# Strassen's algorithm for blocks 1 and 2 in the first layer's a and b products, with a ring of seven weight tiles

## The chip, the cores and the metric

The kernel runs on one core of a Trainium2 chip. The metric is the device time of one execution in microseconds (us); lower is better. Engines: PE (TensorE) multiplies, DVE (VectorE), ACT (ScalarE) and POOL (GpSimd) work on elements, SP (SyncE) issues DMAs. PSUM holds the results of matmuls, SBUF all other tiles.

## The reference

An attention within chunks of 64 tokens, then two layers over 2304 tokens of width 512. Weights of the first layer arrive in 64-bit floats.

```python
x = attention(q, k, v)                        # softmax in chunks of 64, (2304, 512)
x = (x @ w_a) * (x @ w_b) @ w_out             # first layer, d_ff = 1536
p = domain_probs / (domain_probs.sum(-1, keepdims=True) + 1e-09)
for e in range(4):                            # second layer, 4 experts, d_ff = 1024
    out += p[:, e:e+1] * (np.maximum(x @ w1[e], 0) @ w2[e])
```

## The kernel before

Tokens stand in 18 tiles of 128, in five blocks: block 0 has two tiles (256 columns), blocks 1 to 4 have four (512 columns). Each factor of a product is kept as a high and a low float32r part; ACT makes the high part by a cast (`split_hi`), POOL or DVE the low part by a subtraction (`sub_hi`), and one product is three matmuls.

**First layer.** d_ff is cut into 12 chunks f of 128, taken in pairs F = 0 to 5. For a block and a chunk, `ab_steps` makes a (12 matmuls of up to 512 columns), copies it to SBUF (`end_a`, ACT), makes b (12 matmuls), and `end_b` multiplies b out of PSUM by a (DVE) and splits the product g into gh (ACT) and gl (POOL). `x2_steps` then multiplies gh and gl of both chunks by w_out, in four steps (one for each 128 columns of the width) of 6 matmuls, and adds each out of PSUM to the block's sum xacc (DVE). The x2 of a block is put between the steps of the block behind it. F=0 runs in `spans` between the last steps of the attention, F=1 to 5 loop over the blocks in the order 1, 2, 3, 4, 0.

**Weights.** A piece is a 128x512 tile of w_a (0), w_b (1) or w_out (2) of a chunk; it is loaded into one of two raw buffers. `prep_begin` turns the 64-bit words into float32 (`from_f64`): two ACT passes, three DVE passes (L143, L144, L147), a POOL addition (L155), and the next load. `prep_end` splits the result into a tile of the ring `w_p` of eight: ACT cast, POOL subtraction. The places of these steps are written out by hand in `put(u, s, ...)`: behind step s of the u-th block.

**Second layer.** For 16 groups (four experts, four of each), `seq` makes the first product of two blocks by Strassen's algorithm (Winograd's form): 7 half products (`half_mm`, 6 matmuls) in place of 8, from combinations T1 to T4 of the blocks' tiles (B11, B21, B12, B22; `combos`) and sums S1 to S4 of the weights' quarters (`w_sums`), with five additions on DVE that combine the results. The combinations of blocks 1 and 2 are made from xacc in F=5 (`in_turn(in_place(...))`).

Each engine takes its instructions in program order. PSUM has two rings of four buffers: pm for a, b and the Strassen products, ps for x2 and others.

```python
def add_sb(out, in0, in1, op=ALU.add):        # DVE, both inputs in SBUF
    nc.vector.scalar_tensor_tensor(
        out=out, in0=in0, scalar=1.0, in1=in1, op0=ALU.mult, op1=op
    )
```

Of the kernel before, what the change touches and what calls it, by code (L numbers as in the profile page):

```python
# [28 lines left out]
def fused_kernel(  # L29
# [22 lines left out]

    nc = tc.nc
# [17 lines left out]
    w_p = ctx.enter_context(tc.tile_pool(name="w", bufs=8))  # L71
# [6 lines left out]
    st_p = early.enter_context(tc.tile_pool(name="st", bufs=3))  # L78
    late = {}
# [39 lines left out]
    pieces = [(0, f, i) for f in range(2 * NP1) for i in range(3)]  # L119
# [44 lines left out]
    def split_w(src):  # L164
        t = w_tile()
# [91 lines left out]


# [212 lines left out]
    def x2_steps(fs, j, i0, nt):  # L471
# [4 lines left out]
        def step(dd):  # L476
# [98 lines left out]
    def seq(w, t, on):  # L575
# [142 lines left out]
    with tc.manual_schedule():  # L718
# [52 lines left out]
        slots_by = [7, 9, 11, 13, 14, 15, 17, 19, 21, 21, 21]  # L771
        x2 = []
        for r, (f, j, i0, nt) in enumerate(spans):
# [7 lines left out]
            for i, step in enumerate(steps):  # L781
# [6 lines left out]
                if r > 5 and i in (3, 6):  # L788
                    if r in (6, 7):
                        (prep_begin if i == 3 else prep_end)()  # L790
                    elif r == 9 or i == (6 if r == 8 else 3):
                        prep_begin()
                if r == 10 and i in (5, 7):
                    prep_end()
            if r == 3:
                domain_probs()
        early.close()
        late["p"] = ctx.enter_context(tc.tile_pool(name="late", bufs=1))


        for F in range(1, NP1):
            T = {}
# [4 lines left out]
            put(0, 9, prep_end)
            put(0, 10, prep_end)
            if F < NP1 - 1:
                for u, s in ((0, 14), (1, 4), (2, 4), (2, 14), (3, 4), (3, 14)):  # L810
                    put(u, s, prep_begin)
                for u, s in ((1, 10), (1, 14), (4, 6), (4, 12)):
                    put(u, s, prep_end)
            else:
                w_next = w2_steps(0, True)
                for u, s in ((1, 8), (1, 14), (4, 6), (4, 12)):
                    put(u, s, lambda: w_next.pop(0)())
                at = [(1, 10 + 2 * i) for i in range(4)] + [(2, 10 + 2 * i) for i in range(5)]
                at += [(3, 2 * i) for i in range(7)] + [(4, 2), (4, 4)]
                for (u, s), go in zip(at, in_turn(in_place(acc[1], acc[2])), strict=True):  # L820
                    put(u, s, go)
            for u, j in enumerate((1, 2, 3, 4, 0)):
                nt = blocks[j][1]
                steps = [x for f in (2 * F, 2 * F + 1) for x in ab_steps(f, j, 0, nt)]
                for i, go in enumerate(x2):
                    steps.insert((2 if u else 1) * i + (8 if u == 4 else 5), go)
                x2 = x2_steps((2 * F, 2 * F + 1), j, 0, nt)
                for s, step in enumerate(steps):
                    step()
                    for go in T.get((u, s), ()):  # L830
                        go()
# [102 lines left out]
```

## Time and profile before

| | us |
|---|---|
| median of 3 runs (lowest to highest) | 1262.83 (1262.13 to 1263.19) |
| the profiled execution | 1262.41 |
| its span, first to last instruction | 1260.6 |
| PE busy in the span | 1249.0 |
| DVE, ACT, POOL busy | 689.1, 439.1, 326.6 |
| one turn of F (F=2 to 4) | 74.04 |

The profile is one execution. Busy time of an engine doesn't count issuing, branches or semaphores. Idle time is put down to what ended it; idle time of an engine that isn't the last one due costs nothing. Matmuls overlap, so a row's mean time of a matmul is longer than what it adds to a stream of them. In the rows below a is the tile of the first product and of g, gl and gh are its parts, w the weight tiles, t and raw a weight on its way out of 64 bits, s the weight sums.

### The profile page before, as it was taken

Reading aid. Unit: us, or ns where it says so; the run is one execution under the profiler, and the core shown is the slowest. Engines: PE = TensorE matmul, PEld = TensorE weight load, DVE = VectorE, ACT = ScalarE, POOL = GpSimd, SP = SyncE. Lnnn points to the kernel's source line nnn. Section 1 sums busy time; section 2 is a strip of 40 time slices with the busy share of each in tenths; the row PEclk is TensorE's granted clock in tenths of the full one; section 3 lists DMA queues with packets and bytes.
Section 4 is the critical chain, followed back from the end, with each engine's and each line's share of the span. In section 5 each row is a group of like instructions: output and inputs, shape, how many; then the busy total and the mean of one; then the engine's idle time right before and its main releaser. Section 6 shows DMA issues by size and latency. Waiting matters only on the chain.

```text
span 1260.6 us, 17511 instructions
## 1 busy us (share of the span) xinstructions
PE 1249.0 (99%) x6916; PEld 1042.6 (83%) x6916; DVE 689.1 (55%) x1124; ACT 439.1 (35%) x715; POOL 326.6 (26%) x264
## 2 busy tenths in 40 slices
PE   8999999999999999999999999999999999999998
PEld 5887888888888878888888888888888888888887
DVE  7855234343434335566666556665585556555565
ACT  4644422232222223222222232222264444444442
POOL 4523433333343343333333222232320000000000
PEclk9999999999999999999999999999999999999999
DMA  7731211111111100345443454435574444444543
GB/s 259 235 90 57 67 51 34 39 62 34 51 34 51 34 1 1 101 146 201 148 174 134 160 191 158 159 134 183 202 256 161 151 159 158 151 161 140 167 135 132
DMA packets 48033, 156.35 MB, mean 124 GB/s; under 512 B 5456, under 2 KB 5456, under 8 KB 47952
## 3 DMA queue, kind: packets, MB, share of 16 engines
q1 hardware_dynamic: 47952, 155.25, 36.5%
q8 instruction: 54, 0.88, 0.3%
q14 instruction: 27, 0.22, 0.1%
HBM read 100.18 MB, written 55.05 MB: 123 GB/s over the span
## 4 chain that ended last, share of the span: by engine, by line
PE 89%; DVE 0%; POOL 0%; ACT 0%; issue 0%
PE ps L700 31%; PE pm L566 24%; PE pm L452 20%; PE ps L413 5%; PE ps L414 5%; PE ps L415 5%; DVE s L99 0%; POOL cB L107 0%; DVE oacc L687 0%; POOL w L107 0%; POOL gl L107 0%; DVE xacc L95 0%; ACT w L92 0%
## 5 line engine op out<-in xcount | busy, mean ns | idle before, releaser
L700 PE MATMUL ps<-w,h 128*128 128x512 f32 x1536 | 353.4, 389 | 0.0
L700 PEld LDWEIGHTS ps<-w,h 128*128 128x128 f32 x1536 | 288.2, 188 | 59.8
L687 DVE SCALAR_TENSOR_TENSOR oacc<-ps,pr,oacc 128x512 f32<-128x512 f32 x270 | 191.7, 749 | 104.4 <-PE ps L700 104.4
L452 PE MATMUL pm<-xh,w 128*128 128x512 f32 (+1 forms) x976 | 232.6, 367 | 0.0
L452 PEld LDWEIGHTS pm<-xh,w 128*128 128x128 f32 x976 | 172.1, 189 | 30.6
L566 PE MATMUL pm<-cT,w 128*128 128x512 f32 x768 | 184.9, 389 | 0.0
L566 PEld LDWEIGHTS pm<-cT,w 128*128 128x128 f32 x768 | 144.0, 188 | 29.8
L566 PE MATMUL pm<-cB,w 128*128 128x512 f32 x576 | 146.6, 390 | 0.0
L107 POOL TENSOR_TENSOR w<-raw,w 128x512 fp32r<-128x512 f32 x64 | 82.6, 1290 | 203.4 <-ACT w L92 139.4
L452 PE MATMUL pm<-xl,w 128*128 128x512 f32 (+1 forms) x488 | 123.8, 366 | 1.4 <-DVE xl L99 1.4
L566 PEld LDWEIGHTS pm<-cB,w 128*128 128x128 f32 x576 | 107.0, 188 | 21.4
L107 POOL TENSOR_TENSOR gl<-a,gh 128x512 fp32r<-128x512 f32 (+1 forms) x61 | 71.2, 1168 | 188.8 <-ACT gh L92 188.7
L195 ACT CAST w<-kept 128x1024 fp32r<-128x1024 f32 x96 | 98.9, 1045 | 56.5 <-DMA kept<-kept 56.1
L95 DVE TENSOR_TENSOR xacc<-ps,xacc 128x512 f32<-128x512 f32 (+1 forms) x112 | 70.6, 633 | 87.8 <-PE ps L415 87.6
L92 ACT CAST gh<-a 128x512 fp32r<-128x512 f32 (+1 forms) x61 | 34.8, 571 | 198.9 <-DVE a L95 198.9
L452 PEld LDWEIGHTS pm<-xl,w 128*128 128x128 f32 x488 | 87.2, 189 | 16.9 <-DVE xl L99 1.6
L95 DVE TENSOR_TENSOR a<-pm,a 128x512 f32<-128x512 f32 (+1 forms) x61 | 38.4, 629 | 101.3 <-PE pm L452 98.9
L413 PE MATMUL ps<-gl,w 128*128 128x512 f32 (+1 forms) x244 | 90.3, 370 | 2.0 <-POOL gl L107 1.8
L414 PE MATMUL ps<-gh,w 128*128 128x512 f32 (+1 forms) x244 | 89.3, 366 | 0.0
L415 PE MATMUL ps<-gh,w 128*128 128x512 f32 (+1 forms) x244 | 89.0, 365 | 0.0
L155 POOL TENSOR_TENSOR t<-t,raw 128x512 int32<-128x512 int32 x36 | 46.8, 1301 | 86.0 <-issue 38.8
L107 POOL TENSOR_TENSOR w<-s,w 128x512 fp32r<-128x512 f32 x32 | 43.7, 1384 | 73.2 <-ACT w L92 73.2
(87 smaller groups left out, 1333.5 us busy)
## 6 DMA issues: line engine op xcount, KB each, us to landing
kept<-w SPq DMA_DIRECT2D x96, 512.0 KB, 6.2
kept<-kept SPq DMA_DIRECT2D x96, 512.0 KB, 3.2
raw<-in_w1p_dram SPq DMA_DIRECT2D x36, 512.0 KB, 3.5
raw<-in_w2p_dram SPq DMA_DIRECT2D x32, 512.0 KB, 4.6
q<-in_q_dram SPq DMA_DIRECT2D x18, 256.0 KB, 4.3
k<-in_k_dram SPq DMA_DIRECT2D x18, 256.0 KB, 4.7
v<-in_v_dram SPq DMA_DIRECT2D x18, 256.0 KB, 4.4
out_dram<-oacc SPq DMA_DIRECT2D x18, 256.0 KB, 2.0
```

The costliest lines, as they stand in the source:

```text
L92: nc.scalar.copy(out=dst, in_=src)
L95: nc.vector.tensor_tensor(out=out, in0=in0, in1=in1, op=op)
L107: eng.tensor_tensor(out=dst, in0=src, in1=hi.bitcast(F32), op=ALU.subtract)
L155: nc.gpsimd.tensor_tensor(out=t.bitcast(I32), in0=t.bitcast(I32), in1=low.bitcast(I32), op=ALU.add)
L195: nc.scalar.copy(out=t, in_=fetched.pop(key))
L413: nc.tensor.matmul(out=ps[:, :n], lhsT=wh, rhs=al, start=(m == 0), stop=False)
L414: nc.tensor.matmul(out=ps[:, :n], lhsT=wh, rhs=ah, start=False, stop=False)
L415: nc.tensor.matmul(out=ps[:, :n], lhsT=wl, rhs=ah, start=False, stop=(m == last))
L452: nc.tensor.matmul(out=st[i][:, :n], lhsT=x, rhs=y, start=m == 0, stop=m == 3 * KD - 1)
L566: nc.tensor.matmul(out=ps, lhsT=x, rhs=y, start=first and kk == 0 and m == 0, stop=kk == 1 and m == 2, skip_group_check=not first,)
L687: nc.vector.scalar_tensor_tensor(out=o, in0=ps, scalar=p1, in1=o, op0=ALU.mult, op1=ALU.add)
L700: nc.tensor.matmul(out=ps[k], lhsT=x[:, s], rhs=y, start=f == 0 and m == 0, stop=f == 1 and m == 2,)
```

## The change

Blocks 1 and 2 leave the plain loop in F=1 to 5. Their a and b products are made as one pair pass, "A" (`seq_ab`, 14 steps): `seq` runs once for a and once for b, with 7 x 6 matmuls each, its results C11, C22, C21, C12 being chunk and block (the first digit the chunk of the pair, the second the block). `on_b` multiplies; only C11 is still in PSUM then, the other three are in SBUF and take `add_sb`. The x2 of both blocks, eight steps, stand between the steps of the piece behind the pass. The order of the pieces is 3, 4, 0, A in F=1, then 3, 4, A, 0, and A, 3, 4, 0 in F=5. In a plain block the order is a of both chunks, then b of both.

The weights' sums S1 to S4 are made for each F and product (`sums`, four DVE additions of 256 columns) and split (`ent_s`: two ACT casts, two POOL subtractions of 512). The pieces are loaded by kind: a, a, b, b, w_out, w_out of the pair. The combinations T1 to T4 of blocks 1 and 2 are made once, in F=1, from the high and low parts of x (`first_combos`, 16 steps in blocks 3, 4 and 0). The x of blocks 1 and 2 is stored by halves of the width, high and low of each half, as `seq` wants it. The ring of weight tiles has seven tiles in place of eight; a, gl and the Strassen temporaries share a ring `ag` of six, gh has four named tiles, and the T tiles and S tiles lie in a pool `mid` that is opened when the attention's pools close and closed after A in F=5.

```diff
-    w_p = ctx.enter_context(tc.tile_pool(name="w", bufs=8))
+    w_p = ctx.enter_context(tc.tile_pool(name="w", bufs=7))
...
-    pieces = [(0, f, i) for f in range(2 * NP1) for i in range(3)]
+    pieces = [(0, f, i) for f in range(2) for i in range(3)]
+    pieces += [(0, 2 * F + f, i) for F in range(1, NP1) for i in range(3) for f in range(2)]
...
+    def begin_f32(F, i):
+
+        prep_begin()
+        f32s[F, i] = ready[0, 2 * F + i % 2, i // 2]
+
+    def sums(F, m):
+        a1, a2 = f32s[F, 2 * m], f32s[F, 2 * m + 1]
+        f32s[F, "s", m] = w_sums(a1[:, :256], a1[:, 256:], a2[:, :256], a2[:, 256:])
+
+    def ent_s(F, m, i):
+
+        t = late["mid"].tile([P, 2, 512], F32R, tag="S", name="S", bufs=2)
+        split_w(f32s[F, "s", m][i], t)
...
-    def a_tile(dtype=F32, shape=(P, 512)):
-        return g_p.tile(list(shape), dtype, tag="a", name="a", bufs=2)
...
+    def ag_tile(dtype=F32):
+        return g_p.tile([P, 512], dtype, tag="ag", name="ag", bufs=6)
...
+        steps = [
+            lambda: (temps("mT4", "ab"), temps("mT2", "cd"), whole("a", "B12", g)),
+            lambda: whole("b", "B22", g),
+            lambda: minus("c", "b", "a"),
+            later("T3", 0, lambda: two("c"), v),
+            later("T3", 1, lambda: two("c"), v),
+            lambda: whole("d", "B11", v),
+            lambda: minus("a", "a", "d"),
+            later("T1", 0, lambda: two("a"), g),
+            later("T1", 1, lambda: two("a"), g),
+            lambda: minus("b", "b", "a"),
+            later("T2", 0, lambda: two("b"), v),
+            later("T2", 1, lambda: two("b"), v),
+            lambda: whole("a", "B21", v),
+            t4,
+            later("T4", 0, lambda: tmp["e"], g),
+            later("T4", 1, lambda: tmp["e"], g),
+        ]
...
+        def on_b(name, ap):
+            g = ga[name]
+            (add if name == "11" else add_sb)(g, ap, g, ALU.mult)
+            f, j = 2 * F + (name[0] == "2"), int(name[1])
+            gs[f, j, 0] = (gh_tile(name), ag_tile(F32R))
+            to_parts(g, *gs[f, j, 0])
...
+                put(3, 8, prep_end)
+                put(3, 9, lambda: begin_f32(F, 4))
+                put(3, 12, lambda: begin_f32(F, 5))
+                put(3, 14, prep_end)
+                put(4, 1, prep_end)
...
+                    put(3, 11, lambda: begin_f32(F, 4))
+                    put(3, 13, lambda: begin_f32(F, 5))
+                    put(3, 15, prep_end)
+                    put(4, 2, prep_end)
...
+                put(0, 0, lambda: sums(n, 0))
+                put(0, 2, lambda: ent_s(n, 0, 0))
+                put(0, 3, lambda: begin_f32(n, 2))
+                put(0, 4, prep_end)
+                put(0, 5, lambda: ent_s(n, 0, 1))
+                put(0, 6, lambda: begin_f32(n, 3))
+                put(0, 8, prep_end)
+                put(0, 11, lambda: sums(n, 1))
+                put(0, 12, prep_end)
...
-            for u, j in enumerate((1, 2, 3, 4, 0)):
+            for j in ("A", 3, 4, 0) if end else (3, 4, 0, "A") if F == 1 else (3, 4, "A", 0):
+                if j == "A":
+                    steps = seq_ab(F)
+                    after = [2, 3, 4, 5]
```

Two places of the order. On POOL, in F=1 before the change, while blocks 1 and 2 run: gl are low parts of products, w of weight tiles, t the end of a conversion.

```order
L107 TENSOR_TENSOR gl<-a,gh 128x512
L107 TENSOR_TENSOR w<-t,w 128x512 x3
L107 TENSOR_TENSOR gl<-a,gh 128x512
L155 TENSOR_TENSOR t<-t,raw 128x512
L107 TENSOR_TENSOR gl<-a,gh 128x512
L155 TENSOR_TENSOR t<-t,raw 128x512
L107 TENSOR_TENSOR gl<-a,gh 128x512
L107 TENSOR_TENSOR w<-t,w 128x512 x2
L107 TENSOR_TENSOR gl<-a,gh 128x512
L155 TENSOR_TENSOR t<-t,raw 128x512
L107 TENSOR_TENSOR gl<-a,gh 128x512
```

The two w in a row are for the next pair of chunks. After the change, on POOL in F=1 while blocks 3 and 4 run; tmp and cT belong to the combinations, ag to the low parts of products:

```order
L677 TENSOR_TENSOR tmp<-cB_869 128x1024
L677 TENSOR_TENSOR tmp<-cB_870 128x1024
L109 TENSOR_TENSOR w<-t,w 128x512
L158 TENSOR_TENSOR t<-t,raw 128x512
L109 TENSOR_TENSOR ag<-ag,gh 128x512
L158 TENSOR_TENSOR t<-t,raw 128x512
L109 TENSOR_TENSOR w<-t,w 128x512
L109 TENSOR_TENSOR ag<-ag,gh 128x512
L109 TENSOR_TENSOR w<-t,w 128x512
L109 TENSOR_TENSOR cT_2174<-tmp,cT_2174 128x512 x2
L109 TENSOR_TENSOR ag<-ag,gh 128x512 x2
```

The last two rows of w ahead of the cT rows are the w_out tiles of this F, which the x2 of block 3 takes in block 4, with the low part of a product between them; two passes of 1024 and two rows of cT stand around them. On DVE, in F=2 before the change, at the turn from block 1 to block 2 (xacc_873 is the sum of block 1, filled by its x2):

```order
L95 TENSOR_TENSOR a<-pm,a 128x512
L143 TENSOR_SCALAR raw<-raw 128x512
L144 TENSOR_SCALAR t<-t 128x512
L147 SCALAR_TENSOR_TENSOR t<-t,raw 128x512
L95 TENSOR_TENSOR xacc_873<-ps,xacc_873 128x512 x3
L95 TENSOR_TENSOR a<-pm,a 128x512
L95 TENSOR_TENSOR xacc_873<-ps,xacc_873 128x512
L95 TENSOR_TENSOR a<-pm,a 128x512
L143 TENSOR_SCALAR raw<-raw 128x512
L144 TENSOR_SCALAR t<-t 128x512
L147 SCALAR_TENSOR_TENSOR t<-t,raw 128x512
```

One conversion (L143, L144, L147) stands ahead of the first addition to xacc. After the change, at the end of F=2's pair pass and in block 0 behind it (s are weight sums of F=3, xacc_882 is block 1's sum, L101 reads only SBUF, ag<-gh,ag is the end multiplication; L146, L147 and L150 are the L143, L144 and L147 of before):

```order
L101 SCALAR_TENSOR_TENSOR ag<-gh,ag 128x512
L97 TENSOR_TENSOR gh<-gh,ps 128x512
L101 SCALAR_TENSOR_TENSOR ag<-gh,ag 128x512
L97 TENSOR_TENSOR gh<-pm,gh 128x512
L101 SCALAR_TENSOR_TENSOR ag<-gh,ag 128x512
L101 SCALAR_TENSOR_TENSOR s_3033<-t 128x256
L101 SCALAR_TENSOR_TENSOR s_3032<-t 128x256
L101 SCALAR_TENSOR_TENSOR s_3032<-s_3033,t 128x256
L101 SCALAR_TENSOR_TENSOR s_3033<-t,s_3032 128x256
L146 TENSOR_SCALAR raw<-raw 128x512
L147 TENSOR_SCALAR t<-t 128x512
L150 SCALAR_TENSOR_TENSOR t<-t,raw 128x512
```

Three multiplications, four sums and a conversion have come ahead of the first addition to xacc of block 1; the conversion was there before.

## Rows read from the trace of the kernel before

**Rows 1.** The page of the kernel before: busy us of each engine over the span (share, instructions), and the chain that ended last by engine and by line.
```profile
PE 1249.0 (99%) x6916; PEld 1042.6 (83%) x6916; DVE 689.1 (55%) x1124; ACT 439.1 (35%) x715; POOL 326.6 (26%) x264
...
PE 89%; DVE 0%; POOL 0%; ACT 0%; issue 0%
PE ps L700 31%; PE pm L566 24%; PE pm L452 20%; PE ps L413 5%; PE ps L414 5%; PE ps L415 5%; DVE s L99 0%; POOL cB L107 0%; DVE oacc L687 0%; POOL w L107 0%; POOL gl L107 0%; DVE xacc L95 0%; ACT w L92 0%
```

**Rows 2.** The windows of the core: start and end of the stretch, its length, then busy us (and instructions) of PE, PEld, DVE, ACT and POOL, the granted clock of PE, the DMA share and GB/s. The first is in the attention, then F=2 and F=5.
```profile
20.00:40.00 20.00, 17.35 (x286) 14.92 (x290) 18.37 (x40) 9.67 (x19) 12.11 (x12) 0.83 0.72 243
...
219.42:293.46 74.04, 74.04 (x362) 62.68 (x361) 29.41 (x48) 21.16 (x38) 27.15 (x23) 1.00 0.14 43
...
441.54:515.20 73.66, 72.88 (x347) 61.01 (x346) 32.91 (x40) 20.86 (x33) 26.47 (x19) 1.00 0.07 22
```

**Rows 3.** The chain that ended last, in order of time: start, us, engine and line, number of instructions. The first row is a and b products of the first pair of chunks, late in the attention, the second the Strassen pass of one group of the second layer.
```profile
128.78 10.88 PE pm L452 x48
...
542.32 9.55 PE pm L566 x42
```

**Rows 4.** The waits of PE over the whole span: what it waited for, us in total, times, the longest.
```profile
PE ps L413 <- POOL gl L107: 1.8, 3, 0.8
```

**Rows 5.** The groups by form from 121 to 515 us (F=1 to 5 and the end of F=0): busy us, mean ns of one, then the idle time before them and what ended it.
```profile
L107 POOL TENSOR_TENSOR gl<-a,gh 128x512 fp32r<-128x512 f32 x43 | 55.8, 1298 | 135.6 <-ACT gh L92 135.6
L95 DVE TENSOR_TENSOR xacc<-ps,xacc 128x512 f32<-128x512 f32 x80 | 55.2, 690 | 66.0 <-PE ps L415 65.9
...
L107 POOL TENSOR_TENSOR w<-t,w 128x512 fp32r<-128x512 f32 x28 | 35.8, 1293 | 14.3 <-ACT w L92 9.1 <-issue 5.1
...
L95 DVE TENSOR_TENSOR a<-pm,a 128x512 f32<-128x512 f32 x42 | 29.1, 692 | 78.1 <-PE pm L452 75.7 <-ACT a L458 1.7
L92 ACT CAST gh<-a 128x512 fp32r<-128x512 f32 x42 | 26.1, 620 | 169.5 <-DVE a L95 169.5
...
L143 DVE TENSOR_SCALAR raw<-raw 128x512 uint32<-128x512 uint32 x27 | 19.1, 707 | 53.8 <-ACT t L141 53.7
L147 DVE SCALAR_TENSOR_TENSOR t<-t,raw 128x512 uint32<-128x512 uint32 x27 | 18.7, 692 | 0.9
...
L144 DVE TENSOR_SCALAR t<-t 128x512 f32<-128x512 f32 x27 | 11.3, 417 | 0.0
...
L107 POOL TENSOR_TENSOR gl<-a,gh 128x256 fp32r<-128x256 f32 x10 | 7.4, 737 | 30.6 <-ACT gh L92 30.6
...
L107 POOL TENSOR_TENSOR cB<-xacc,cB 128x1024 fp32r<-128x1024 f32 x2 | 5.0, 2494 | 0.0
...
L99 DVE SCALAR_TENSOR_TENSOR xacc<-xacc,xacc 128x1024 f32<-128x1024 f32 x3 | 3.7, 1217 | 0.0
...
L99 DVE SCALAR_TENSOR_TENSOR s<-s,raw 128x256 f32<-128x256 f32 x1 | 0.4, 411 | 0.0
```

**Rows 6.** The page's costliest groups: low parts of weight sums in the second layer and in F=5.
```profile
L107 POOL TENSOR_TENSOR w<-s,w 128x512 fp32r<-128x512 f32 x32 | 43.7, 1384 | 73.2 <-ACT w L92 73.2
```

**Rows 7.** The timeline in F=2: start, us, engine, line, instruction, and the idle time before it with its releaser. Words of a weight (raw, t) on DVE beside the low part of a product on POOL.
```profile
223.02 1.29 POOL L107 TENSOR_TENSOR gl<-a,gh 128x512 fp32r<-128x512 f32 x1 [3.26 <-ACT gh L92]
...
223.54 1.06 DVE L143 TENSOR_SCALAR raw<-raw 128x512 uint32<-128x512 uint32 x1 [1.25 <-ACT t L141]
...
224.52 0.41 DVE L144 TENSOR_SCALAR t<-t 128x512 f32<-128x512 f32 x1
```

**Rows 8.** The timeline in the second layer, same columns.
```profile
559.48 2.39 DVE L99 SCALAR_TENSOR_TENSOR gl<-xacc,xacc 128x512 f32<-128x512 f32 x2
559.88 3.14 POOL L107 TENSOR_TENSOR w<-s,w 128x512 fp32r<-128x512 f32 x2 [4.73 <-ACT w L92]
```

**Rows 9.** The timeline of F=5 at the wait of 0.78 us, same columns.
```profile
460.10 1.29 POOL L107 TENSOR_TENSOR gl<-a,gh 128x512 fp32r<-128x512 f32 x1 [5.77 <-ACT gh L92]
...
460.57 3.64 DVE L99 SCALAR_TENSOR_TENSOR s<-raw 128x256 f32<-128x256 f32 x2
...
461.35 2.59 POOL L107 TENSOR_TENSOR cB<-xacc,cB 128x1024 fp32r<-128x1024 f32 x1
...
464.14 0.41 DVE L99 SCALAR_TENSOR_TENSOR s<-s,raw 128x256 f32<-128x256 f32 x1
...
464.58 0.62 ACT L92 CAST w<-s 128x512 fp32r<-128x512 f32 x1 [3.61 <-DVE s L99]
...
465.28 1.30 POOL L107 TENSOR_TENSOR w<-s,w 128x512 fp32r<-128x512 f32 x1 [1.35 <-ACT w L92]
...
466.54 2.40 POOL L107 TENSOR_TENSOR cB<-xacc,cB 128x1024 fp32r<-128x1024 f32 x1
...
468.89 1.28 POOL L107 TENSOR_TENSOR gl<-a,gh 128x512 fp32r<-128x512 f32 x1
...
470.23 0.50 PE L413 MATMUL ps<-gl,w 128*128 128x512 f32 x1 [0.78 <-POOL gl L107]
```

**Rows 10.** The timeline of PE from 20 to 26.5 us, the rows with idle time before them, same columns.
```profile
20.27 0.69 PE L287 MATMUL pm<-k,q 64*64 64x64 f32 x32 [0.79 <-DMA k<-in_k_dram]
...
23.87 0.39 PE L452 MATMUL pm<-xl,w 128*128 128x256 f32 x1 [1.37 <-DVE xl L99]
...
24.82 0.74 PE L287 MATMUL pm<-k,q 64*64 64x64 f32 x30 [0.31 <-DVE d L299]
26.05 0.69 PE L322 MATMUL ps<-ident,d 128*128 128x128 f32 x2 [0.49 <-POOL d L316]
```

More of the change, by code (lines that the diff above doesn't have):

```diff
@@ L162, in w_tile, with split_w @@
         return w_p.tile([P, 2, 512], F32R, tag="w", name="w")
[L164 to L165 removed]
+    def split_w(src, t=None):
+        t = w_tile() if t is None else t
         split_hi(t[:, 0, :], src)
@@ L651, in emit_h0 @@
         w = wts[1, g]
-        hh, hl = (a_tile(F32R, (P, 2, B0)) for _ in range(2))
-        h, l = xp[0]
+        hh, hl = (late["p"].tile([P, 2, B0], F32R, tag=n, name=n) for n in ("hh0", "hl0"))
+        h, l = xp[0][0]
         for f, names in enumerate((("A11", "A12"), ("A21", "A22"))):
@@ L787, in fused_kernel @@
                     x_lo_rest()
[L788 to L794, printed above, removed]
+                for go in T.get((r, i), ()):
+                    go()
             if r == 3:
                 domain_probs()
-        early.close()
@@ L822, in fused_kernel @@
-            for u, j in enumerate((1, 2, 3, 4, 0)):
[L823 to L827, printed above, removed]
+                at = [(3, 11 + i) for i in range(4)] + [(3, 15), (4, 0), (4, 2), (4, 4), (4, 6)]
+                at += [(4, 8), (4, 10), (4, 12), (4, 14), (4, 15)] + [(0, 2 * i + 1) for i in range(4)]
@@ new lines, in fused_kernel @@
+            for j in ("A", 3, 4, 0) if end else (3, 4, 0, "A") if F == 1 else (3, 4, "A", 0):
+                if j == "A":
+                    steps = seq_ab(F)
+                    after = [2, 3, 4, 5]
+                else:
+                    nt = blocks[j][1]
+                    s0, s1 = (list(ab_steps(f, j, 0, nt)) for f in (2 * F, 2 * F + 1))
+                    steps = s0[:4] + s1[:4] + s0[4:] + s1[4:]
+                    first = 4 if j == 3 else 5
+                    after = [min(first + i * (1 if j == 3 else 2), 14) for i in range(len(x2))]
+                    if j == 0:
+                        after = [5 + i * (1 if len(x2) > 4 else 2) for i in range(len(x2))]
+                if end and j == 3:
+                    place = dict(B11="s1", B21="s2", T3="s3", T2="s4", T1="s5", T4="s6", B22="s7")
+                    for (u, s), go in zip(at, in_turn(in_place(acc[1], acc[2])), strict=True):
+                        put(u, s, go)
@@ L833, in fused_kernel @@
+                if end and j == "A":
+                    mid.close()
+                    late["p"] = ctx.enter_context(tc.tile_pool(name="late", bufs=1))
         side = []
```

189 lines of the change are left out of this document (148 added, 41 removed).

## The prediction

> **What bounds the kernel now.** I read the page's busy shares and its chain by engine first [rows 1]: TensorE (PE) is busy 99% of the span and holds 89% of the chain, so in every stage matmuls set the end, and a change pays by taking matmuls away or costs by making PE wait. The windows of one turn of the loop F come next [rows 2]: F=2 takes 74.04 us with PE busy all of it, GpSimd (POOL) 27.15 and VectorE (DVE) 29.41; only F=5 has a hole, 73.66 us with 72.88 busy. A 512-column matmul costs its stream time: 48 in a row take 10.88 us, which is 226.7 ns each, and the Strassen pass of the second layer, which is what the change brings in here, runs at the same price, 9.55 for 42 [rows 3]. The waits say how thin the cover is: PE waits for low parts out of POOL three times, 1.8 us in all, 0.8 at most [rows 4]. So POOL's queue is the second in line, although it is busy only 37% of a turn.
>
> **The saving.** For each F from 1 to 5 and for each of a and b, blocks 1 and 2 take 7 half products of 6 matmuls, 42, where 2 chunks x 2 blocks x 12 = 48 stood. That is 12 fewer in an F and 60 in all, at 226.7 ns: **-13.6 us**. A turn becomes 74.04 - 2.72 = 71.3 us. The price is sure, since both forms of the matmul run at it [rows 3]; nothing else is removed from PE. All other edits (three stores of x by halves, renamed tiles, the order of loads) change no count on PE, and with 1.00 granted clock and DMA shares of 0.07 to 0.14 in these windows [rows 2] I cost the loads at nothing: the two raw buffers are reloaded as before, some 6 per F.
>
> **What is added beside PE.** Durations are from the groups by form [rows 5]. In an F: eight weight sums of 256 columns on DVE (0.41 each, 3.3), three end multiplications that now read only SBUF instead of PSUM (0.69 each), ten more additions out of PSUM (0.69), four casts on ACT (0.62) and four low parts of sums on POOL. For those the nearest row is w<-s, 1.38 on the page's mean [rows 6]; 5.5 us. Once, in F=1 and its way in, the combinations T1 to T4 are made: on POOL two whole additions of 1024 columns (2.5 each, as cB) and four lows of 512 (1.29), on DVE five passes of 1024 (1.22) and six of 512. POOL's sum for a turn is then 27.15 + 5.5 = 32.7 of 71.3 us; DVE's grows from 29.4 to about 40 (ten additions 6.9, the sums 3.3). By busy time alone all of this hides, and the saving would stand nearly whole. The question is whether it comes in time.
>
> **DVE and POOL take turns.** A DVE instruction that reads only SBUF does not run beside one of POOL. Where POOL starts the low part gl at 223.02 for 1.29 us, DVE's mask (L143), due at 223.54, takes 1.06 in place of the 0.4 that its twin L144 takes next, and ends 0.29 after POOL's end [rows 7]. Two subtractions of 512 columns take 2.39 while POOL makes two w, and these take 3.14 in place of 2.58 [rows 8]; two sums of 256 take 3.64, not 0.83, while POOL makes gl and then cB [rows 9]. The additions out of PSUM stay at 0.69 in every group [rows 5]. So per turn one more account must be kept, POOL's time plus that of DVE's SBUF-only work: before, 27.15 + 6 conversions x (0.42 + 0.42 + 0.69) = 36.4 of 74.0; after, 32.7 + 9.2 + 3.3 + 2.1 = 47.3 of 71.3, from 49% to 66%, with peaks.
>
> The Trainium skill says the same more sharply ("SBUF — State Buffer", section "SBUF: two separate sides"): the pair of ports that the two engines share is a lock held for the whole instruction, against VectorE instructions with two SBUF inputs or in a two-port mode, and whoever comes second stands still. The trace agrees with 1.06 for 0.4. The mean says less: all 27 masks L143 average 0.707, 0.29 too much, and L144 and L147 behind them lose nothing [rows 5]. By the rule at every meeting the waits below come out whole; by the mean, the 17 instructions of an F that can be met (6 masks, 8 sums, 3 multiplications) lose 0.29 each, 5 us of DVE time that is mostly hidden, and the sum would stay near rival 1.
>
> **Where PE will wait.** I followed the queues in the order of the instructions, with the durations above and hand-overs of 0.02 to 0.08 us (DVE ends at 464.55, ACT starts 464.58; ACT ends 465.20, POOL 465.28; POOL ends 470.17, PE 470.23) [rows 9].
>
> (a) F=2, 3, 4, the end of the pair pass and block 0 behind it (16.6 us of PE): POOL has nine instructions of 1.29 and one of 0.74, 12.4 us; DVE has SBUF-only one multiplication, eight sums and two conversions, 7.1: 19.5 us of turns in 16.6. At the pass's end (E) the addition c22 is done at E-1.5, but POOL holds a w low part until E-0.9; multiplication of chunk 22 to E-0.2, PSUM addition to E+0.5, multiplication of 21 to E+1.2, POOL's low of 22 to E+2.5, multiplication of 12 to E+3.2, and only then the low part of 21, to E+4.5. PE wants it in the first x2 step at E+2.8: 1.7 us. Then four sums and a conversion stand on DVE ahead of the first addition into xacc1, each behind one POOL instruction; they end near E+11.3, and the fifth x2 step needs that PSUM buffer at E+10.7: 0.6, and the seventh much the same. I take 2.5 each, 7.5; without turns 0.2 each; at most 3.2.
>
> (b) F=1, block 4: x2 of block 3 needs the two w_out tiles. Their conversions stand behind the 2.5 us passes of the combinations, and on POOL the order is w, gl, w with three DVE passes of the combinations between them. PE waits for w, then gl, then w. With turns I get 5.3 (7.0 if PE's last copies leave as late as they may), without them 2 to 3.1.
>
> (c) F=2, block 4: again both w_out tiles, prepared only at steps (3,15) and (4,2), since everything for chunk pair 2 is converted in block 3 (POOL ten instructions of 1.29, 12.9; DVE SBUF-only eight sums and four conversions, 9.4: 22.4 us of turns in 21.8 of PE): 3.1 with turns and 3.0 without, as POOL's own queue is the limit.
>
> (d) Smaller: the way in, spans r=9 and 10, where 16.4 us of turns stand in 16.3 of PE, 1.4; F=1 block 0, 0.6; F=2 block 3, the low of 21 behind a w, 1.6; F=5, where 0.78 is waited already behind two cB lows [rows 9], 1.0 more for the copy of m1 and the lows.
>
> Sum: 7.5 + 5.3 + 3.1 + 1.4 + 0.6 + 1.6 + 1.0 = **+20.5**. Net 20.5 - 13.6 = +6.9. On the profiled execution's 1262.41 (span 1260.6 and 1.8 around it) that is 1269.3, on the median 1262.83 1269.7: **1269.5**.
>
> The ring of seven in place of eight w tiles takes a lead of one tile away; a w low would be held until PE leaves an older tile. Along my queues that release was always earlier than POOL's turn, so I take 0; if not, one wait of 1.3 per F, 6 us in all, is the upper bound.
>
> **Rivals.** (1) *The turns are mostly absorbed.* PE's waits are only those that POOL's queue makes by itself: (b) 2 to 3.1, (c) 3.0, the rest 0.2 each for three and about 1: 6.6. Time 1262.8 - 13.6 + 6.6 = **1255.8**, faster. For it: L144 and L147 lose nothing and PE doesn't wait in F=2 to 4 before, at 49%. Against: 19.5 and 22.4 us of turns in stretches of 16.6 and 21.8. It decides by whether (a) and (b) wait less than 13.6 - 6.6 = 7 us beyond this.
> (2) *Half.* Turns delay, but stretches before with slack absorb half of (a), (b), (d): waits of 13.5 and **1262.7**, within 0.2%.
> (3) *My forecast*, slower, through (a) to (d).
> (4) *The clock.* Behind waits of 0.79, 1.37, 0.31 and 0.49 us between 20 and 26 us [rows 10] the granted clock averages 0.83 over 20 to 40 us [rows 2]: (1 - 0.83)/0.5 of 20 us = 6.8 us at the lower level, which costs 3.4. (b) is such a string, three waits within 1 us of matmuls. With one or two such falls **1273 to 1276**.
> The Trainium skill bears on it ("TensorE: Matmul & The Clock Gate", section "A second HAM failure mode: psum-queue depth-cycling"): frequent short idle times between groups of matmuls let the clock fall and rise. Waits of 0.8 in this trace did not do it: F=5 has 0.78 and a clock of 1.00 [rows 2].
> That the saving doesn't come is no rival: the count of matmuls falls by 60 by the code.
>
> **How the numbers follow.** Forecast 0.40 (1266 to 1272.5), rival 1 0.38 (1252 to 1259.5), rival 2 0.15, rival 4 0.07. 0.2% (2.5 us) is about what a measurement of this kernel can tell; the three runs of before lie within 1.1. Faster by over 0.2%: rival 1 and a little of rival 2, 0.40; within: 0.12; slower: forecast, rival 4 and the rest, 0.48. The range reaches from rival 1 with fewer waits, 1253, to rival 4, 1277.
>
> **What would show it.** PE x60 fewer and matmul time 13.6 less in any case. In the windows, F=3 and 4 at about 73.8 us (right), 71.5 (rival 1). In the waits, PE for POOL's ag (the lows) and w, and for DVE's xacc, some 20 us in place of 1.8; in the groups by form, L143 and the weight sums of 256 near 1 us in place of 0.42 to 0.71. F=1, block 4, with three waits of 1.5 to 2 in a row. Wrong would be sums of 0.45 and PE busy above 99% in F=3; a clock below 1.00 in F=1 or 2 is rival 4.

## The result

| | us |
|---|---|
| before, median of 4 runs | 1262.64 |
| after, median of 4 runs (lowest to highest) | 1276.49 (1276.11 to 1277.23) |
| ratio after to before, 95% interval | 1.011 [1.0093, 1.0128] |
| predicted | 1269.5, range 1253 to 1277 |

The change is slower, as forecast, by 13.9 us where the working had 6.9. The profiled execution after took 1277.23, its span is 1275.5; so the two profiled executions lie 14.8 us apart.

The page after, busy shares and the chain by engine, as [rows 1]:

```profile
PE 1244.9 (98%) x6856; PEld 1032.1 (81%) x6856; DVE 781.6 (61%) x1233; ACT 451.8 (35%) x746; POOL 376.7 (30%) x290
...
PE 83%; DVE 10%; POOL 3%; issue 2%; ACT 1%; DVEq 0%; ACTq 0%; POOLq 0%
```

60 matmuls are gone (x6916 to x6856), but DVE and POOL now hold 13% of the chain, where they stood at 0%. PE's waits, as [rows 4] (us, times, the longest):

```profile
PE ps L445 <- POOL ag L109: 11.7, 11, 1.5
PE ps L447 <- POOL w L109: 4.8, 4, 2.2
PE ps L445 <- DVE xacc L97: 2.9, 3, 1.0
...
PE ps L445 <- ACT w L94: 0.6, 1, 0.6
```

20.0 us in place of 1.8, all in front of x2 (L445 to L447). The windows, as [rows 2]: F=1 block 4, F=2 block 4, the end of F=2's pass with block 0, then the turns of F=3 and of F=4, block 3 to block 0:

```profile
160.00:172.00 12.00, 7.67 (x22) 5.14 (x21) 7.58 (x7) 3.35 (x6) 7.37 (x5) 0.72 0.15 44
240.00:252.00 12.00, 9.79 (x34) 7.02 (x33) 2.38 (x4) 2.73 (x5) 5.00 (x4) 0.86 0.32 89
285.00:303.00 18.00, 15.64 (x84) 12.95 (x83) 16.68 (x24) 7.00 (x14) 13.21 (x11) 1.00 0.19 58
303.79:378.22 74.43, 72.21 (x349) 60.24 (x348) 44.55 (x64) 22.67 (x41) 35.19 (x27) 1.00 0.15 43
378.22:451.73 73.51, 71.27 (x346) 59.57 (x345) 44.64 (x68) 22.81 (x41) 33.60 (x26) 1.00 0.15 44
```

A turn takes 74.43 and 73.51 us; 74.04 stood before [rows 2], the working had 73.8 for these, and the matmuls alone would take 71.3. In the first two stretches the granted clock is 0.72 and 0.86. The groups by form from 121 to 530 us, as [rows 5]:

```profile
L109 POOL TENSOR_TENSOR ag<-ag,gh 128x512 fp32r<-128x512 f32 x43 | 63.1, 1476 | 95.7 <-ACT gh L94 95.7
L97 DVE TENSOR_TENSOR xacc<-ps,xacc 128x512 f32<-128x512 f32 x80 | 53.6, 685 | 66.1 <-PE ps L447 65.8
...
L109 POOL TENSOR_TENSOR w<-t,w 128x512 fp32r<-128x512 f32 x29 | 41.9, 1448 | 4.2 <-ACT w L94 4.1
...
L150 DVE SCALAR_TENSOR_TENSOR t<-t,raw 128x512 uint32<-128x512 uint32 x28 | 26.3, 938 | 1.0
...
L147 DVE TENSOR_SCALAR t<-t 128x512 f32<-128x512 f32 x28 | 20.5, 731 | 0.0
...
L101 DVE SCALAR_TENSOR_TENSOR s<-t 128x256 f32<-128x256 f32 x20 | 17.1, 893 | 1.6 <-POOL t L158 1.6
L146 DVE TENSOR_SCALAR raw<-raw 128x512 uint32<-128x512 uint32 x28 | 16.5, 588 | 21.0 <-ACT t L144 20.9
L101 DVE SCALAR_TENSOR_TENSOR ag<-gh,ag 128x512 f32<-128x512 f32 x15 | 15.9, 1061 | 0.5
```

Here the turns are to be seen. In the mean, DVE's instructions on SBUF have grown: L147 0.417 to 0.731, L150 0.692 to 0.938, sums of 256 columns 0.411 to 0.893, the multiplications 1.061 where one out of PSUM takes 0.69. The mask L146, which was the one that suffered before (0.707), fell to 0.588; the turn now falls on the two behind it, not on it as I had written. Those out of PSUM have not (xacc 0.690 to 0.685). POOL's low parts went from 1.298 to 1.476, w from 1.293 to 1.448: it waits for DVE as DVE waits for it.

These means mix two kinds of instruction, and the traces keep them apart. Before, 15 of the 27 masks ran while POOL was idle and took 0.43 each; the other 12 overlapped with an instruction of POOL and took 1.05. L144 and L147 of before met none, which is why they lost nothing. After, 12 of the 28 L147 and 7 of the 28 L150 met POOL and took 1.15 and 1.68, against 0.42 and 0.69 for the rest.

The timeline at the end of F=2's pass, DVE and POOL with some rows left out, then PE:

```profile
282.39 1.74 POOL L109 TENSOR_TENSOR w<-t,w 128x512 fp32r<-128x512 f32 x1
...
283.61 1.07 DVE L101 SCALAR_TENSOR_TENSOR ag<-gh,ag 128x512 f32<-128x512 f32 x1
...
284.09 4.85 POOL L109 TENSOR_TENSOR ag<-ag,gh 128x512 fp32r<-128x512 f32 x3
...
285.32 1.07 DVE L101 SCALAR_TENSOR_TENSOR ag<-gh,ag 128x512 f32<-128x512 f32 x1
...
286.31 2.92 DVE L101 SCALAR_TENSOR_TENSOR s<-t 128x256 f32<-128x256 f32 x2
```

```profile
285.81 0.39 PE L447 MATMUL ps<-gh,w 128*128 128x512 f32 x1
287.57 0.50 PE L445 MATMUL ps<-ag,w 128*128 128x512 f32 x1 [1.37 <-POOL ag L109]
...
297.07 0.51 PE L492 MATMUL pm<-xh,w 128*128 128x256 f32 x3
298.57 0.50 PE L445 MATMUL ps<-ag,w 128*128 128x512 f32 x1 [0.99 <-DVE xacc L97]
```

The first multiplication (283.61) takes 1.07 and ends 0.55 behind POOL's w (282.39 + 1.74 = 284.13); three low parts take 4.85 in place of 3.9, two sums 2.92 in place of 0.82. PE has issued the third matmul of the first x2 at 285.81 and the next starts at 287.57, not at 286.04: **1.53 us are lost**, of which the profile shows 1.37 as idle, since a matmul's modelled end lies 0.16 behind the start of the next in a stream. I count the rest of the losses like that, start to start, at 0.2267 a matmul of 512 columns (0.12 of 256), and add the 0.1 by which the first matmul behind a wait takes longer (0.50 in place of 0.39).

The other place is F=1 block 4, PE, DVE and POOL:

```profile
160.00 3.24 DVE L101 SCALAR_TENSOR_TENSOR cT<-tmp,cT 128x512 fp32r<-128x512 f32 x2
...
160.97 1.72 POOL L109 TENSOR_TENSOR w<-t,w 128x512 fp32r<-128x512 f32 x1
...
162.66 1.70 POOL L109 TENSOR_TENSOR ag<-ag,gh 128x512 fp32r<-128x512 f32 x1
...
162.75 0.50 PE L447 MATMUL ps<-gh,w 128*128 128x512 f32 x1 [2.19 <-POOL w L109]
163.16 2.28 DVE L677 TENSOR_TENSOR tmp<-cB 128x1024 f32<-128x1024 f32 x1
164.32 2.24 POOL L109 TENSOR_TENSOR w<-t,w 128x512 fp32r<-128x512 f32 x1
...
164.41 0.79 PE L445 MATMUL ps<-ag,w 128*128 128x512 f32 x1 [1.16 <-POOL ag L109]
...
166.62 0.80 PE L447 MATMUL ps<-gh,w 128*128 128x512 f32 x1 [0.98 <-POOL w L109]
...
167.21 1.05 PE L492 MATMUL pm<-xl,w 128*128 128x512 f32 x2
...
168.07 1.91 PE L492 MATMUL pm<-xh,w 128*128 128x512 f32 x4
...
169.77 0.63 PE L445 MATMUL ps<-ag,w 128*128 128x512 f32 x1
```

PE waits for w, ag, w in a row, 2.19, 1.16 and 0.98; w, ag and w take 1.72, 1.70 and 2.24 of POOL beside DVE's combinations (3.24 for two, 2.28). From the second wait on single matmuls last 0.79 in place of 0.39 to 0.50, and the four behind 168.07 take 1.70 to the next row's start at 169.77 (0.91 at the full clock): the lower level of the clock, which is there before the third wait.

### The profile page after: what moved, and what is told of

Its sections match the earlier page's. It is cut to its first block, busy times and chain, and to the rows that moved or that the text cites. A ratio compares the mean times of both kernels' runs of the same rounds, so it can differ in the third digit from the quotient of the medians.

```text
span 1275.5 us, 17604 instructions
## 1 busy us (share of the span) xinstructions
PE 1244.9 (98%) x6856; PEld 1032.1 (81%) x6856; DVE 781.6 (61%) x1233; ACT 451.8 (35%) x746; POOL 376.7 (30%) x290
## 4 chain that ended last, share of the span: by engine, by line
PE 83%; DVE 10%; POOL 3%; issue 2%; ACT 1%; DVEq 0%; ACTq 0%; POOLq 0%
PE ps L830 31%; PE pm L605 28%; PE pm L492 9%; PE ps L445 4%; PE ps L447 4%; PE ps L446 4%; PE ps L605 2%; DVE t L147 1%; POOL ag L109 1%; DVE t L150 1%; DVE raw L146 1%; DVE s L101 1%; DVE ag L101 1%; DVE d L326 1%; DVE xacc L97 1%
## 5 line engine op out<-in xcount | busy, mean ns | idle before, releaser
L605 PE MATMUL pm<-cB,w 128*128 128x512 f32 x696 | 177.2, 390 | 0.0
L605 PEld LDWEIGHTS pm<-cB,w 128*128 128x128 f32 x696 | 129.4, 188 | 26.1 <-POOL cT L109 0.2
L492 PE MATMUL pm<-xh,w 128*128 128x512 f32 (+1 forms) x576 | 134.8, 358 | 0.0
L109 POOL TENSOR_TENSOR ag<-ag,gh 128x512 fp32r<-128x512 f32 (+1 forms) x61 | 79.4, 1308 | 129.1 <-ACT gh L94 128.9
L492 PEld LDWEIGHTS pm<-xh,w 128*128 128x128 f32 x576 | 100.6, 191 | 17.2
L445 PE MATMUL ps<-ag,w 128*128 128x512 f32 (+1 forms) x244 | 92.2, 378 | 15.5 <-POOL ag L109 11.7
L447 PE MATMUL ps<-gh,w 128*128 128x512 f32 (+1 forms) x244 | 90.3, 370 | 4.8 <-POOL w L109 4.8
L94 ACT CAST gh<-ag 128x512 fp32r<-128x512 f32 (+1 forms) x61 | 34.9, 572 | 161.5 <-DVE ag L97 129.8
L492 PE MATMUL pm<-xl,w 128*128 128x512 f32 (+1 forms) x288 | 73.2, 359 | 0.9 <-DVE xl L101 0.9
L445 PEld LDWEIGHTS ps<-ag,w 128*128 128x128 f32 x244 | 46.3, 190 | 28.6 <-POOL ag L109 16.1
L97 DVE TENSOR_TENSOR ag<-pm,ag 128x512 f32<-128x512 f32 (+1 forms) x61 | 38.1, 625 | 50.2 <-PE pm L492 38.9
```

The source lines that it names most:

```text
L94: nc.scalar.copy(out=dst, in_=src)
L97: nc.vector.tensor_tensor(out=out, in0=in0, in1=in1, op=op)
L109: eng.tensor_tensor(out=dst, in0=src, in1=hi.bitcast(F32), op=ALU.subtract)
L445: nc.tensor.matmul(out=ps[:, :n], lhsT=wh, rhs=al, start=(m == 0), stop=False)
L447: nc.tensor.matmul(out=ps[:, :n], lhsT=wl, rhs=ah, start=False, stop=(m == last))
L492: nc.tensor.matmul(out=st[i][:, :n], lhsT=x, rhs=y, start=m == 0, stop=m == 3 * KD - 1)
```

## The experiments

Times are medians; the kernel before, measured again beside each of them, lay at 1262.4 to 1262.9, and a ratio with its 95% interval is to that. Unless said, an edit is made on the changed kernel (1276.5).

**e1, the multiplications read PSUM.**

```diff
-        add(t["c22"], pd, t["u3"])
+        c22 = pc if in_ps else t["c22"]
+        add(c22, pd, t["u3"])
...
-            (add if name == "11" else add_sb)(g, ap, g, ALU.mult)
+            add(g, ap, g, ALU.mult)
```

(and C21 into pe, C12 into pd, for b alone)

> The b product's C22, C21 and C12 are added up in PSUM (in the banks of their last operands) in place of SBUF, so that the three end multiplications read one operand from PSUM; as many instructions of the same size on every engine. Turn-taking theory: these multiplications no longer wait for POOL, so the waits of PE for the low part of 21 behind the pass (1.73 in F=2 block 3, 1.63, 1.53 and 1.54 in F=2 to 4 block 0, measured as lost start-to-start time) go, and those for xacc (1.24, 1.22, 1.24) shrink, since the additions queue up earlier: 6 to 10 us less than the changed kernel, 1267 to 1270. Rival (POOL's queue of low parts is by itself too long, whatever DVE reads): within 1.5 us of 1276.5.

1270.38, ratio to before 1.0065 [1.005, 1.008]: 6.1 less, at the edge of what the turns would give and far from the rival. At the same place as above:

```profile
279.78 0.69 DVE L97 TENSOR_TENSOR ag<-pm,ag 128x512 f32<-128x512 f32 x1
...
280.49 1.30 POOL L109 TENSOR_TENSOR w<-t,w 128x512 fp32r<-128x512 f32 x1
...
281.11 0.69 DVE L97 TENSOR_TENSOR ag<-ps,ag 128x512 f32<-128x512 f32 x1
...
281.75 3.99 POOL L109 TENSOR_TENSOR ag<-ag,gh 128x512 fp32r<-128x512 f32 x3
...
282.44 0.69 DVE L97 TENSOR_TENSOR ag<-pm,ag 128x512 f32<-128x512 f32 x1
283.05 2.97 DVE L101 SCALAR_TENSOR_TENSOR s<-t 128x256 f32<-128x256 f32 x2
```

The multiplications (279.78, 281.11, 282.44) take 0.69 beside a busy POOL, and the three lows come at 3.99 in a row. The first wait is gone in F=2 (there and in block 3, 0.28), 3 and 4. Nothing but the place of an operand was changed, so the turns are the cause of those waits, not the length of POOL's queue. The waits for xacc hardly shrank (1.12, 1.10, 1.10, from 1.24, 1.22, 1.24): PE, too, comes earlier. That part of the expectation was wrong.

**e2, x2 later in block 4 of F=1 and 2.**

```diff
-                    first = 4 if j == 3 else 5
+                    first = 4 if j == 3 else 8 if j == 4 and F < 3 else 5
```

> In block 4 of F=1 and 2 alone, the four x2 steps of block 3 stand behind steps 8, 10, 12, 14 in place of 5, 7, 9, 11, some 2.7 us later. Theory: the w_out tiles are late by a fixed time, so F=2 (3.3 us lost to waits, 1.6 more at the lower clock) loses nothing, F=1 (5.9 and 1.6) about 3: 8 to 9.5 less, 1267 to 1268.5, and the granted clock stays 1.00 in F=2 block 4. Rival (the lower clock is not due to these waits): the waits shrink but 3 us of lower clock stay, 1270 to 1271.5. Rival (the w tiles are held by the ring of seven until x2 steps run, so they move along): no change.

1270.42 [1.0049, 1.0079]: 6.1 less, 1.9 to 3.4 short of the expectation. The windows:

```profile
158.00:170.00 12.00, 9.20 (x29) 6.55 (x29) 9.02 (x7) 3.35 (x6) 9.40 (x6) 0.77 0.15 44
238.00:250.00 12.00, 11.52 (x50) 8.91 (x49) 3.42 (x6) 3.28 (x6) 6.22 (x5) 1.00 0.30 89
```

F=2's block 4 is nearly mended (waits of 0.20 and 0.28) and its clock stays at 1.00. In F=1 only the first of the three waits went: the w tiles come one after the other as POOL and DVE alternate, and a later start doesn't change the distance between them. The third even grew from 0.98 to 1.47, and more matmuls run at the lower clock, which costs some 2.6 in place of 1.5. Where the waits stayed, the lower clock stayed (0.77); where they went, it went. The rival of the ring falls as well: no cast and no low part of a w tile waits for PE around these steps.

**e3, both.** 

> Both edits, e1 and e2. If the two groups of waits are independent the gains add up: 1258 to 1262, at or below the kernel before (1262.6). If the queues only pass the delay on, less than the sum, 1265 or more.

1266.11 [1.0016, 1.0038], 10.4 less. That is above the range for independent gains and in the one for queues that pass the delay on, 1.8 more than the sum of the two would leave (1264.3). But its runs spread from 1263.7 to 1266.9, and the profiled executions do add up: spans of 1275.5 after the change, 1270.5 for e1, 1270.1 for e2, 1265.1 for both. So 1266.1 doesn't show that a delay is passed on; the sum was set too low, since e2 gave less than expected.

**e6, low parts of the sums on DVE.**

```diff
-        split_w(f32s[F, "s", m][i], t)
+        split_w(f32s[F, "s", m][i], t, nc.vector)
```

> The low parts of the weight sums (four of 512 columns in an F) move from POOL (1.36 each) to DVE (0.69 each, SBUF only). Turn-taking theory: the turns of an F fall by 5.5 - 2.8 = 2.7 us, but DVE's queue ahead of the xacc additions gets longer: F=2 block 4 loses 1 to 3 us less, the three waits for xacc grow by up to 1: 1272 to 1276. Rival (POOL's own queue is what is too long): 5.5 us less on it per F takes most waits in F=2 to 5 away, 1264 to 1267.

1275.49 [1.0087, 1.0121]. Taking 5.5 us per F off POOL gains almost nothing, which speaks against POOL's length as the cause. In detail I was wrong: the xacc waits did not grow but fell from 1.24 to 0.38 lost (why was not tested); a new one of 1.04 came in F=2 block 3. Block 4 of F=2 shows a limit of what was read from the clock above:

```profile
240.00:252.00 12.00, 10.12 (x43) 7.40 (x42) 2.76 (x5) 2.73 (x5) 5.01 (x4) 1.00 0.30 89
```

There are three waits in a row here as well (0.21, 1.39 and 0.28, where the changed kernel had 0.56, 1.39 and 0.26), and the granted clock is 1.00 and not 0.86. Three waits in a row do not always bring the lower level.

**e10, the sums made once.**

```diff
     def sums(F, m):
+        if (F, m) != (1, 0):
+            return
```

(`ent_s` the same, and `left` takes the tiles of F=1)

> The changed kernel, with the weight sums made only once (a product of F=1) and used for every F and product, so that the product is another one: eight DVE additions of 256 columns, four ACT casts and four POOL low parts fewer in an F; the matmuls, multiplications and combinations stay. Turn-taking theory: 14.7 -> 11.3 us of DVE's SBUF-only work and 32.7 -> 27.2 of POOL's, the xacc waits (1.24, 1.22, 1.24) and F=2 block 4 (3.3 and 1.6) go, the first wait behind the pass, which hangs on the multiplications and low parts, stays (4 x 1.5) or halves, F=1 block 4 (7.5) stays: 1266 to 1269. Rival (the sums are hidden and do not matter): 1275 to 1277.

1267.83 [1.0023, 1.005]: the xacc waits are gone, two of the first waits behind the pass stay and two are halved (1.47, 0.66, 1.42, 0.65), F=1 block 4 stays. Block 4 of F=2 stays too (3.0 lost to waits, 3.3 in the changed kernel), which I had expected to go: it hangs on the conversions in block 3. The wait at F=1's start (1.69) went too. The sums' own share is thus the xacc waits, that one and half of two first waits. This run takes work off both POOL and DVE, so by itself it can't tell the turns from POOL's length; e6, with the same low parts off POOL, can.

The next three stand on e3 (1266.1).

**e7, the low parts of a's sums on DVE for F=3 to 5.** 

> The kernel of the run with both edits (1266.1), and the low parts of the a product's weight sums of F=3, 4 and 5 (two of 512 columns each, made in block 0) on DVE in place of POOL. The waits for xacc in block 0 (1.10, 1.12, 1.12) fall to 0.4 as they did when all low parts of sums moved, and nothing is added in F=2 block 3: 1263.5 to 1264.5. Rival (with less ahead of it DVE's queue is now the limit there): 1265.5 to 1267.

1264.19 [1.0, 1.0018], as expected, though the three waits lose 0.39, 0.67 and 0.40.

**e8, w_out ahead of the combinations in F=1.**

```diff
-        put(10, 6, lambda: sums(1, 1))
...
-                put(3, 8, prep_end)
-                put(3, 9, lambda: begin_f32(F, 4))
-                put(3, 12, lambda: begin_f32(F, 5))
-                put(3, 14, prep_end)
-                put(4, 1, prep_end)
-                at = [(3, 1), (3, 4), (3, 11), (3, 13), (3, 15), (4, 3), (4, 5), (4, 7), (4, 9)]
+                put(3, 1, prep_end)
+                put(3, 2, lambda: sums(1, 1))
+                put(3, 4, lambda: begin_f32(F, 4))
+                put(3, 6, lambda: begin_f32(F, 5))
+                put(3, 9, prep_end)
+                put(3, 11, prep_end)
+                at = [(3, 5), (3, 8), (3, 12), (3, 14), (4, 0), (4, 3), (4, 5), (4, 7), (4, 9)]
```

> The kernel with both edits (1266.1), and in F=1 the w_out tiles are converted ahead of the combinations: the last w_b tile at step (3,1), the sums of b at (3,2) in place of the last span, w_out from (3,4), split at (3,9) and (3,11), the first combinations five steps later. Nothing is left out and the counts stay. Theory (order of the queue, not the amount): the three waits in F=1 block 4 (0.34, 1.44, 1.63, and 1.2 at the lower clock behind them) go, and the wait at F=1's start (1.69) falls below 0.5: 1260 to 1262. Rival (F=1 has too much work for POOL and DVE in turns, 67 of 71 us): the waits move to the combinations, PE waits at the pass of F=1 and the time stays within 1.5 of 1266.

1259.2 [0.9961, 0.9983], 6.9 less than e3 and below the kernel before. The stretch that had a clock of 0.72:

```profile
157.00:169.00 12.00, 11.67 (x52) 9.35 (x51) 10.50 (x10) 4.91 (x10) 8.52 (x6) 1.00 0.00 1
```

Block 4 has one wait of 0.33 for a low part left and the clock is 1.00, with the same instructions: in F=1 the order of the queue was at fault, not the amount of work.

**e9, e7 and e8 together.** 

> Both of these edits on the kernel with the first two: if they are independent 1257.5 to 1260, below the kernel before (1262.6) by 0.2 to 0.4%. If F=1's work only moves on, 1263 or more.

1256.82 [0.9941, 0.9968]: the gains add up.

**e13, e9 without the edit of e1.** 

> The kernel of 1256.8 with the end multiplications reading SBUF again (the first edit taken back alone). Turn-taking theory: the four waits behind the pass come back at 1.5 each, some of it in place of the xacc waits that follow: +4.5 to +6.5, 1261.3 to 1263.3. Rival (with the queues ordered there is slack for the turns): +2 at most, 1257 to 1259.

1262.01 [0.9987, 1.0005], 5.2 more than e9, as the turns would have it. The four waits are back (1.61, 1.54, 1.44 and 1.45 lost). The price of the three SBUF operands shows at a second place, with everything else in order.

**e11, the kernel before with x by halves.**

```diff
-        h, l = xp[j]
-        split_hi(h[:, :, s], ps)
+        n = KD // len(xp[j])
+        for m, (h, l) in enumerate(xp[j]):
+            p = ps[:, n * m : n * m + n, :]
+            split_hi(h[:, :, s], p)
```

(low parts and `kparts` likewise)

> The kernel before, with one part of the change alone: the x of blocks 1 and 2 is stored by halves of the width (high of half 1, low of half 1, then half 2), so that a token tile of them takes two casts and two subtractions of 256 columns in place of one of 512. Theory: this is what the attention lost (the wait for a low part at 38 us grew from 0.21 to 1.07, and three waits for copies of xacc came in place of one): +1 to +1.8, 1263.8 to 1264.6. Rival (the ring that a, gl and the temporaries share is what made these waits): no change, within 0.4 of 1262.8.

1263.92, ratio 1.0011 [1.0003, 1.002], 1.3 more. Of this, 0.3 lies outside the span (2.1 us around it in the median run, 1.8 before and after): the spans' medians are 1261.8 and 1260.8, so inside it the halves cost 1.0. PE's waits:

```profile
PE ps L417 <- POOL gl L107: 2.7, 3, 1.1
...
PE ps L363 <- ACT xacc L493: 1.0, 3, 0.4
```

The wait for gl at 38 us is 1.08 as after the change (0.21 before), and the three waits for ACT's copies are there.

**e12, x2 in block 0 one step later, on e9.**

```diff
-                        after = [5 + i * (1 if len(x2) > 4 else 2) for i in range(len(x2))]
+                        after = [(6 + i if len(x2) > 4 else 5 + 2 * i) for i in range(len(x2))]
```

(and in F=2 block 4 one step later still)

> The best kernel so far (1256.8), with the x2 behind the pair pass in block 0 one step later, and the x2 in F=2 block 4 one step later than there. The waits that are left there (0.37, 0.66, 0.39 for xacc; 0.41 and 0.44 for the w_out tiles, with some of the lower clock) go: 1255 to 1256.2. Rival (each only moves to the next step): 1256.5 to 1257.5.

1260.18 [0.9971, 0.9989], 3.4 more than e9, against both expectations. DVE and PE in F=2's block 0:

```profile
277.10 0.94 DVE L146 TENSOR_SCALAR raw<-raw 128x512 uint32<-128x512 uint32 x1
277.95 1.52 DVE L147 TENSOR_SCALAR t<-t 128x512 f32<-128x512 f32 x1
279.50 0.69 DVE L150 SCALAR_TENSOR_TENSOR t<-t,raw 128x512 uint32<-128x512 uint32 x1
280.11 2.48 DVE L97 TENSOR_TENSOR xacc<-ps,xacc 128x512 f32<-128x512 f32 x4
```

```profile
280.86 0.50 PE L445 MATMUL ps<-ag,w 128*128 128x512 f32 x1 [1.55 <-DVE xacc L97]
```

The additions into xacc moved behind the second conversion in DVE's order, so they wait for it, 1.55 us where 0.22 to 0.52 stood. Here what stands ahead counts, not the distance in time.

**e14, the conversions behind the additions, on e9.**

```diff
-                put(0, 3, lambda: begin_f32(n, 2))
+                put(0, 5, lambda: begin_f32(n, 2))
...
-                put(0, 6, lambda: begin_f32(n, 3))
+                put(0, 7, lambda: begin_f32(n, 3))
```

(with the later x2 of e12 in F=2 block 4)

> The kernel of 1256.8, with the x2 in F=2 block 4 one step later (which took 0.6 us of waits away), the x2 in block 0 where they were, and the two conversions in block 0 at steps 5 and 7 in place of 3 and 6, so that DVE's first addition into xacc of block 1 stands ahead of a conversion instead of behind it. Theory (what an addition out of PSUM waits for is the SBUF-only work queued ahead of it, three instructions and their turns, about 1.5 to 3 us for each conversion): the waits for xacc (0.37, 0.66, 0.39) go and nothing comes in their place: 1254.7 to 1256.0. Rival (the delay only moves to the weight tile of the conversion or to the next addition): 1256.5 to 1259.

**1254.36** (1253.77 to 1254.7), ratio to before 0.9935 [0.9921, 0.9948], 0.3 below what was expected; no wait for xacc is left in its trace. The turn of F=3:

```profile
286.48:358.33 71.85, 71.85 (x350) 60.23 (x348) 42.22 (x65) 22.72 (x41) 31.25 (x25) 1.00 0.16 45
```

PE is busy for all of 71.85 us, where 74.43 stood after the change and 74.04 before. This is the saving of the prediction, 2.72 an F less 0.5. The same algorithm, with the queues in another order, three operands in PSUM and some low parts of sums on DVE, is 22 us faster than the changed kernel and 8 faster than the one before.

## Why the prediction was right in kind and half in size

The bound (PE), the saving (60 matmuls; the turn of e14) and the places of the waits were right. Of the causes, the turns are shown for the first waits of (a) and for F=2 block 3 in (d): e1 and e13 take them away and bring them back by the place of an operand alone. The waits for xacc hang on the SBUF work that stands ahead on DVE (e10, e12, e14). (b) goes with another order of the same instructions (e8), and so does (c) with a later use (e2); the way in of (d) goes with e8 and e10. The other two of (d), F=1 block 0 and F=5, were not tested. That POOL's own queue is the limit in (c), as the prediction had it, is at best part of it: with 5.5 us an F less on POOL it still lost 2.7 of 3.3 to waits (e6).

Term by term, lost start to start, less what before lost at the same place:

| term | predicted | measured |
|---|---|---|
| saving | -13.6 | -13.6 (by the count; e14's turn agrees within 0.5) |
| (a) F=2, 3, 4 block 0 | 7.5 | 8.4 (1.63 + 1.24, 1.53 + 1.22, 1.54 + 1.24) |
| (b) F=1 block 4 | 5.3 | 5.9 |
| (c) F=2 block 4 | 3.1 | 3.3 |
| (d) the smaller four | 4.6 | 4.8 (1.6, 0.75, 1.7, 0.7) |
| the lower clock behind (b) and (c) | 0 | 2.7 (1.5 and 1.2) |
| x by halves, attention | 0 | 1.0 (e11, span) |
| sum | +6.9 | +12.5 of 13.9 |

**The step that failed** is the sum, in two terms that I set to zero. First the clock: I made it rival 4, as if it were another case than my own, at a chance of 0.07. It was no rival but came with (b) and (c): a forecast with such waits in a row should have carried a price for it. It came to 1.5 and 1.2 us a fall, less than the 3.4 that I had taken from the attention (and than the 1.6 each in the expectations of e2 and e10). The 1276.5 measured lies just above rival 4 (1273 to 1276), and within the range of 1253 to 1277 only because that reached to rival 4's end. Second, "all other edits change no count on PE", taken as no cost: the stores by halves cost 1.0 us, since DVE's and ACT's counts do change there. The waits themselves were 1.9 too low in sum, 0.9 of it in (a). 1.4 us of the medians' difference, and 2.3 of the profiled executions' 14.8, from which the waits are read, stay without a place that I could name; part of it is spread over losses of 0.16 and below. One sum of the prediction is off without effect: 27.15 and six conversions of 1.53 make 36.3, not 36.4.

The rule of the Trainium skill on the shared ports, that the pair is held for a whole instruction ("SBUF — State Buffer", section "SBUF: two separate sides"), which I weighed against the mean of 0.29 for each meeting, came out whole: 0.48 more for a sum of 256 and 0.37 for a multiplication are means over meetings and misses alike. So was the 0.29: it stood for 12 masks that lost 0.63 each and 15 that met nothing. An estimate by that mean would have stayed near rival 1.

Of the Trainium skill's rule on the clock, that frequent short idle times between groups of matmuls let it fall and rise ("TensorE: Matmul & The Clock Gate", section "A second HAM failure mode: psum-queue depth-cycling"), the traces show both sides. The lower level came with the second of the waits of 2.19, 1.16 and 0.98 (a mean of 0.72 in F=1 block 4) and with the third of 0.56, 1.39 and 0.26 (0.86 in F=2 block 4). It did not come with 0.21, 1.39 and 0.28 (e6), nor with single waits of 1.37 and 0.99 with 10 us of matmuls between (1.00 from 285 to 303).

The ring of seven, taken at 0, was not tried by itself. But in the traces after the change and of e14 no cast and no low part of a w tile waits for PE in F=1 to 5, as it would if the ring held it back; so 0 was right as far as the traces show.

## What to carry to other kernels

Keep a further account beside each engine's busy time: what VectorE does on SBUF alone plus all of GpSimd's time. Where it nears the length of a stage, try moving an operand to PSUM before you move work to another engine (6.1 us here against 1.0, e1 and e6), and put what frees the tensor engine (additions out of PSUM, the low part that is due first) ahead of conversions in program order. When a duration is a mean, ask how many of its instructions met the other engine. When a forecast holds several waits in a row, add a price for a fall of the clock to it (1.2 and 1.5 us here).

## What was not expected of the hardware

GpSimd pays for the turns as well: low parts of 512 columns took 1.476 in the mean in place of 1.298, a single w 2.24. A wait of PE costs more than the idle time that the profile shows, 0.16 that the modelled end hides and 0.1 on the next matmul, some 5 us over the 18 waits for POOL's tiles and for xacc. And DVE's whole-tile passes of 1024 columns that met POOL took 2.28 in place of 1.22.
